# First expert's last weight piece split in two blocks, and the second expert's first eight gathers issued in one run

## The chip, the core and the metric

One NeuronCore of a Trainium2 chip runs the whole kernel. Its engines are TensorE (PE, with its weight loads as PEld), VectorE (DVE), ScalarE (ACT), GpSimd (POOL) and SyncE (SP, which only issues transfers here). Each engine runs its own instructions strictly in the order in which the program lists them, and waits for the others through semaphores. The metric is the device time of one execution in microseconds; the time given for a kernel is the median of its timed runs.

## What is computed

A decayed (retention) attention over 4 batches, 8 heads, 768 positions and head size 64, whose output is read as 3072 tokens of 512 numbers, and then a mixture of 8 experts in which each token goes to the expert with the highest logit:

```python
def _moe_ref(x, w_gate, w_output_gate, w1, w2):       # x: 3072 x 512, the attention's output
    logits = x @ w_gate
    e_idx = np.argmax(logits, axis=1)
    ...                                               # gate_w: the softmax of the chosen expert; eom: an output gate
    for e in range(E):
        mask = e_idx == e
        h = np.maximum(x[mask] @ w1[e], 0.0)
        ye = h @ w2[e]
        out[mask] = gate_w[mask, None] * eom[mask, e, None] * ye
```

Everything is in float32, and the experts' products are made to that accuracy.

## The kernel before

**Precision.** An expert's matrix product is three TensorE products: each operand is held as a high part (`...hi`, rounded to TensorE's fast float32 form) and a low part (`...lo`, the rest), and `mm3` (lines 85 to 87) adds hi x hi, lo x hi and hi x lo. So each block of weights, of tokens and of hidden values is split before use: ACT makes the high part (`split_hi`, line 132, tile `whi`; `x_hi`, line 982, `xhi`; the relu of line 1061, `hhi`), and DVE the low part by a subtraction (`split_lo2`, line 146, `wlo`; `x_lo`, line 986, `xlo`; line 1062, `hlo`).

**Weights.** An expert's two matrices come as four pieces of 1 MB (`load_piece`, line 119, tile `raw`, three buffers): pieces 0 and 1 are the halves of the first expert's w1, pieces 2 and 3 those of its w2, piece 4 the first of the second expert. In this document a piece's tiles carry its number: `wlo_2` is the low part of piece 2. `split_lo2(i, h)` makes half h of piece i's low part. SP issues a piece when its buffer is free.

**Tokens.** The experts are ordered by how many tokens they got. Each expert's tokens are fetched from DRAM by gathers on POOL (`gather`, line 951: one indirect DMA of 128 rows for each 32 tokens, tile `xg`), whose row numbers DVE makes (`row_index`, lines 920 and 925, from an index table that SP loads); DVE turns them (`x_turn`, line 968, tile `y`), and the split makes `xhi` and `xlo`. The second expert needs 14 gathers.

**The first expert.** Its tokens come in two parts, columns 0 to 191 (`h = 0`) and 192 to 447 (`h = 1`), since the last tokens are routed late. The hidden values are 8 chunks (fc = 0 to 7) of 12 matmuls for each part (tile `ph`), then the output rows (`down_rows_mm`, tile `pyr`) of 24 matmuls for each block of rows: each fc takes one matmul each of `whi`, `wlo` and `hlo` (lines 85, 86, 87), fc 0 to 3 from piece 2 and fc 4 to 7 from piece 3. The work of part 0 is the list `units`; `fill(n)` issues its next n entries on TensorE between other work, and the relus that follow a chunk are kept back until `settle()` issues them. So between `fill` and `settle` calls the code fixes by hand where splits, relus, row numbers and gathers stand on ACT, DVE and POOL; TensorE's own order doesn't depend on it. Lines 1455 to 1478 are that stretch for the end of part 0: it issues the relus of chunks 4 to 7, the splits of piece 3 and the last half of piece 2, the second expert's row numbers and its first six gathers. Then part 1 runs as a loop over fc, in which each step also issues one further gather of the second expert (`next_rows`); ahead of such a gather POOL copies one number out of the step's fresh `hhi` (`pace`, line 913, tile `beat`), so that a gather waits for its step. The two scatters of the first expert's finished rows (`send_rows`, line 1178) stand on POOL too, where `emit_rows` is called.

**The second expert** begins with `ph_None` (all its columns at once), so all of its tokens must be gathered, turned and split by then. From there on each expert's weights and tokens are fetched and split during the one before.

Of the kernel before, what the change touches and what calls it, by code (L numbers as in the profile page):

```python
# [9 lines left out]
F32 = mybir.dt.float32  # L10
# [13 lines left out]
def kernel(  # L24
# [28 lines left out]
    FIRST = 192  # L53
# [67 lines left out]
    def split_hi(i, j):  # L121
        if i >= len(pieces):
            return
        if pieces[i] not in wparts:
            wparts[pieces[i]] = (
                wpool.tile([P, 4, 512], F32R, tag="whi", bufs=4, name=f"whi_{i}"),
                wpool.tile([P, 4, 512], F32R, tag="wlo", bufs=4, name=f"wlo_{i}"),
            )
        src, hi = raws[i][:, j, :], wparts[pieces[i]][0][:, j, :]
        if turned_out(i):  # L130
            src, hi = by_quarter(src), by_part(hi)
        nc.scalar.copy(out=hi, in_=src)  # L132
# [10 lines left out]
    def split_lo2(i, h):  # L143
        sl = slice(2 * h, 2 * h + 2)
        hi, lo = (t[:, sl, :] for t in wparts[pieces[i]])
        nc.vector.tensor_tensor(out=lo, in0=raws[i][:, sl, :], in1=hi.bitcast(F32), op=ALU.subtract)  # L146
# [794 lines left out]
    def gather(p, b0=0, b1=None, rows=NT):  # L941
        if p >= E:
            return
        for b in range(b0, NB[p] if b1 is None else min(b1, NB[p])):
            i, m = x_place(p, b)
            if (p, i) not in xg and p == 0 and i < 2:
                both = wpool.tile([P, 4, 512], F32, tag="whi", bufs=4, name="xg_0")
                xg[(0, 0)], xg[(0, 1)] = both[:, 0, :], both[:, 1, :]
            if (p, i) not in xg:
                xg[(p, i)] = slot(f"xg_{p}_{i}")  # L950
            nc.gpsimd.indirect_dma_start(  # L951
                out=xg[(p, i)][:, m * P : (m + 1) * P],
                out_offset=None,
                in_=x_q[0 : 4 * rows],
                in_offset=bass.IndirectOffsetOnAxis(ap=gis[(p, b)], axis=0),
                bounds_check=4 * rows - 1,
                oob_is_err=False,
            )
# [77 lines left out]
    hts = {}  # L1036
# [222 lines left out]
    def settle():  # L1259
        while acts:  # L1260
            acts.pop(0)()

    def fill(count):
        for _ in range(min(count, len(units))):
            mm, act = units.pop(0)
            mm()
            if act:
                acts.append(act)

    with tc.manual_schedule():  # L1270
# [181 lines left out]
        load_rows(1)  # L1452
        load_outs0()
        expert_regs(2, order_i[:, 2:E], E - 2)
        for h in range(2):
            split_hi(3, 2 * h)
            split_hi(3, 2 * h + 1)
            fill(8)
            settle()
            if h == 0:  # L1460
                split_lo2(2, 1)
        for h in range(2):
            split_lo2(3, h)
            fill(2)
        row_index(1)
        gather(1, 0, 4)
        split_late()
        settle()
        load_piece(5)
# [4 lines left out]
            x_split(0, g, 1)  # L1474
        fill(4)
        settle()
        gather(1, 4, 6)
        fill(8)
        settle()
        assert not units  # L1480
# [15 lines left out]
        for p in range(E):  # L1496
# [5 lines left out]
            for fc in range(NFC):  # L1502
                if p == 0:
                    up(p, fc, 1)
                    next_rows(1, 6 + fc, 7 + fc, hts[(p, fc)][0][0:1, FIRST : FIRST + 1].bitcast(F32))
                    if fc >= 4:
                        next_split(4, (fc - 4,))
                    if fc >= 5:
                        for f in work[:2]:
                            f()  # L1510
                        work = work[2:]
                else:
                    up(p, fc)
                    next_split(4 * p + 2, (fc,))

                    if fc == 1 and p in TURNED:
                        out_index(p)
                    if fc == 3 and p == E - 1:
                        count_over()
                    if fc >= 4:  # L1520
                        for f in work[: (fc - 2) // 2]:
                            f()
                        work = work[(fc - 2) // 2 :]
                if fc == 3 and p in TURNED:
                    down_banks(p)
                if p == 1:
                    b = 4 + (fc if fc < 6 else 2 * fc - 6)
                    next_rows(2, b, b + 1 + fc // 6, hts[(p, fc)][0][0:1, 0:1].bitcast(F32))
                if p > 1 and fc < 4:
                    b = 4 * 2 if p - 1 in TURNED else 3 * 2  # L1530
                    n = (14 - b + 3) // 4
                    next_rows(p + 1, b + n * fc, b + n * fc + n, hts[(p, fc)][0][0:1, 0:1].bitcast(F32))
                if fc == 0:
                    load_outs(p + 1)
                    load_rows(p + 2)
                if p - 1 in TURNED:
                    if fc == 2:
                        fetch_turned(p - 1)
                    if fc >= 5:
                        send_turned(p - 1, fc - 5)  # L1540
# [32 lines left out]
    with tc.If(anyover > 0):  # L1573
        with tc.tile_pool(name="opool", bufs=1) as opool:
            for p in range(E):
                n_p = nc.values_load(over_i[0:1, p : p + 1], min_val=0, max_val=(NT + P - 1) // P - OVER[p])
                e = bass.ds(nc.values_load(order_i[0:1, p : p + 1], min_val=0, max_val=E - 1), 1)
                with tc.For_i(0, n_p, 1) as i:
# [30 lines left out]
                    for half in range(2):  # L1609
                        ph = bank("o_ph")  # L1610
                        for f in range(4):
                            fc = 4 * half + f
# [55 lines left out]
```

## Time and profile before

| | |
|---|---|
| median of 3 timed runs | 425.43 us (422.97, 425.43, 425.44) |
| the profiled execution's own time | 424.38 us |
| its span, first to last instruction | 422.7 us (1.68 us lie around it) |
| TensorE busy | 403.0 us, 95% |
| DVE busy | 286.5 us, 68% |
| POOL busy | 238.5 us, 56% |
| ACT busy | 189.5 us, 45% |
| attention and routing | to about 120 us of the span |
| first expert | about 120 to 174 us |
| seven more experts | about 175 to 419 us |

Times in a trace count from the span's start. A busy share is an average over stages: what a change in one stage is worth is read from the waits in that stage. A timeline row gives an instruction's start, its duration, its engine and line, what it writes and reads, how many instructions the row joins, and in brackets how long the engine had been idle before it and what ended that. In rows the piece and expert numbers of a tile are left out: `wlo` stands for any piece's.

### The profile page before, as it was taken

What the parts mean: (1) busy time and instruction counts of PE and PEld (TensorE: products, weight loads), DVE (VectorE), ACT (ScalarE), POOL (GpSimd) and SP (SyncE); (2) the same over time, 40 slices, a digit from 0 to 9 for tenths busy, and PEclk for the clock granted to TensorE, in tenths of its full rate; (3) what the DMA queues carried; (4) which work ended last, traced back from release to release, by engine and by line L of the source; (5) the groups of instructions that cost most, each with busy time, mean ns of one, the idle gap of its engine ahead of it and who ended that gap; (6) DMA issues with size and microseconds to landing.
All of it is one profiled execution on the core that took longest, in us unless ns stands there. A gap on an engine that the chain in (4) does not pass through costs nothing.

```text
span 422.7 us, 10572 instructions
## 1 busy us (share of the span) xinstructions
PE 403.0 (95%) x3869; PEld 368.1 (87%) x3869; DVE 286.5 (68%) x810; ACT 189.5 (45%) x460; POOL 238.5 (56%) x301
## 2 busy tenths in 40 slices
PE   6999989989999899999999999999999999999994
PEld 3888878878788597799999999999999989989983
DVE  2758696877789536767865966965884874874710
ACT  4766556665574125344324604703633542542400
POOL 5276678658955777567575467457187266211012
PEclk9999999999999999999999999999999999999999
DMA  8989898889925851465458557946865885361001
GB/s 180 226 230 242 221 256 229 213 236 253 358 69 140 268 181 37 139 212 174 136 158 261 191 181 174 341 131 190 287 214 157 265 287 174 126 222 46 5 26 50
DMA packets 95326, 79.11 MB, mean 187 GB/s; under 512 B 58668, under 2 KB 70992, under 8 KB 95264
## 3 DMA queue, kind: packets, MB, share of 16 engines
q1 hardware_dynamic: 88336, 64.88, 52.1%
q0 software_dynamic: 6208, 12.93, 9.7%
q8 instruction: 32, 0.52, 0.5%
q10 hardware_dynamic: 720, 0.53, 0.5%
q14 instruction: 30, 0.25, 0.2%
HBM read 62.25 MB, written 16.45 MB: 186 GB/s over the span
## 4 chain that ended last, share of the span: by engine, by line
PE 81%; DVE 8%; DMA 5%; another core or an unknown queue 1%; issue 1%; ACT 1%; SPq 0%; POOL 0%; POOLq 0%; DVEq 0%; ACTq 0%
PE ph_None L85 10%; PE ph_None L86 10%; PE ph_None L87 9%; PE py L85 6%; PE py L87 6%; PE py L86 6%; PE pyr L86 4%; PE pyr L87 4%; PE pyr L85 4%; PE ps L401 4%; PE po L476 4%; DMA qkv<-in_k_dram 3%; PE pk L342 2%; PE po L426 2%; PE ph L87 2%; PE pq L342 2%
## 5 line engine op out<-in xcount | busy, mean ns | idle before, releaser
L951 POOL DMA_INDIRECT xg<-x_d,rows x100 | 111.3, 1113 | 60.9 <-issue 33.0
L1061 ACT ACTIVATE hhi<-ph_None 128x400 fp32r<-128x400 f32 (+4 forms) x56 | 28.1, 501 | 113.7 <-PE ph_None L87 81.6
L85 PE MATMUL ph_None<-xhi,whi 128*128 128x400 f32 (+4 forms) x224 | 76.4, 341 | 0.9 <-ACT xhi L982 0.9
L132 ACT CAST whi<-raw 128x512 fp32r<-128x512 f32 x128 | 74.7, 617 | 4.2 <-DMA raw<-in_moe_w_dram 4.2
L86 PE MATMUL ph_None<-xlo,whi 128*128 128x400 f32 (+4 forms) x224 | 76.4, 341 | 0.0
L87 PE MATMUL ph_None<-xhi,wlo 128*128 128x400 f32 (+4 forms) x224 | 76.3, 341 | 0.0
L141 DVE TENSOR_TENSOR wlo<-raw,whi 128x512 fp32r<-128x512 f32 x112 | 74.3, 684 | 0.6 <-ACT whi L132 0.5
L1062 DVE SCALAR_TENSOR_TENSOR hlo<-ph_None,hhi 128x400 fp32r<-128x400 f32 (+4 forms) x56 | 31.6, 565 | 39.7 <-ACT hhi L1061 26.4
L85 PE MATMUL py<-hhi,whi 128*128 128x400 f32 (+2 forms) x128 | 44.6, 348 | 0.0
L86 PE MATMUL py<-hlo,whi 128*128 128x400 f32 (+2 forms) x128 | 44.6, 348 | 0.0
L87 PE MATMUL py<-hhi,wlo 128*128 128x400 f32 (+2 forms) x128 | 44.6, 348 | 0.0
L85 PEld LDWEIGHTS ph_None<-xhi,whi 128*128 128x128 f32 x224 | 42.1, 188 | 1.7 <-ACT xhi L982 1.3
L1178 POOL DMA_INDIRECT out_dram<-yn,table x12 | 12.6, 1048 | 53.5 <-DVE yn L1242 36.6
L86 PEld LDWEIGHTS ph_None<-xlo,whi 128*128 128x128 f32 x224 | 42.1, 188 | 0.6 <-DVE xlo L986 0.2
L87 PEld LDWEIGHTS ph_None<-xhi,wlo 128*128 128x128 f32 x224 | 42.1, 188 | 0.3
L411 DVE TENSOR_TENSOR at<-ps,decay 128x512 f32<-128x512 f32 x48 | 31.1, 682 | 13.2 <-PE ps L401 8.8
L86 PE MATMUL pyr<-wlo,hhi 128*128 128x512 f32 (+2 forms) x96 | 37.6, 392 | 1.8 <-DVE wlo L146 1.8
L346 ACT COPY qT<-pq 64x256 f32<-64x256 f32 x96 | 37.7, 393 | 1.7 <-PE pq L342 0.7
L85 PE MATMUL pyr<-whi,hhi 128*128 128x512 f32 (+2 forms) x96 | 37.5, 390 | 0.0
L87 PE MATMUL pyr<-whi,hlo 128*128 128x512 f32 (+2 forms) x96 | 37.4, 390 | 0.0
L713 POOL DMA_INDIRECT tab_d<-rec,idx x24 | 26.6, 1107 | 14.1 <-issue 9.7
L982 ACT CAST xhi<-y 128x256 fp32r<-128x256 f32 (+3 forms) x64 | 19.5, 357 | 31.5 <-DVE y L968 22.4
(237 smaller groups left out, 784.3 us busy)
## 6 DMA issues: line engine op xcount, KB each, us to landing
raw<-in_moe_w_dram SPq DMA_DIRECT2D x32, 1024.0 KB
x_d<-xn SPq DMA_DIRECT2D x22, 256.0 KB
qkv<-in_k_dram SPq DMA_DIRECT2D x40, 128.0 KB
qkv<-in_v_dram SPq DMA_DIRECT2D x20, 256.0 KB
qkv<-in_q_dram SPq DMA_DIRECT2D x36, 128.0 KB
yd<-yo SPq DMA_DIRECT2D x12, 256.0 KB
yr<-yd SPq DMA_DIRECT2D x48, 64.0 KB
xg<-x_d,rows POOLq DMA_INDIRECT x100
```

Of the source, the lines that this page charges most:

```text
L85: nc.tensor.matmul(ps, a[0], b[0], start=first, stop=False)
L86: nc.tensor.matmul(ps, a[0], b[1], start=False, stop=False)
L87: nc.tensor.matmul(ps, a[1], b[0], start=False, stop=last)
L132: nc.scalar.copy(out=hi, in_=src)
L141: eng.tensor_tensor(out=lo, in0=src, in1=hi.bitcast(F32), op=ALU.subtract)
L346: copies = [lambda r=r, view=view, src=src: nc.scalar.copy(out=view(qT[r]), in_=src) for r, view, src in query_parts(pq)]
L411: nc.vector.tensor_tensor(out=at, in0=ps.rearrange("p (g t) -> p g t", g=NPAIR), in1=dec[:, j], op=ALU.mult)
L713: ins = nc.gpsimd.indirect_dma_start(out=tab_d, out_offset=bass.IndirectOffsetOnAxis(ap=idx, axis=0), in_=rec, in_offset=None, bounds_chec ...
L951: nc.gpsimd.indirect_dma_start(out=xg[(p, i)][:, m * P : (m + 1) * P], out_offset=None, in_=x_q[0 : 4 * rows], in_offset=bass.IndirectOffs ...
L982: nc.scalar.copy(out=hi, in_=src)
L1061: nc.scalar.activation(out=hi[:, r], in_=ph[:, r], func=AF.Relu)
L1062: nc.vector.scalar_tensor_tensor(out=lo[:, r], in0=ph[:, r], scalar=0.0, in1=hi[:, r].bitcast(F32), op0=ALU.max, op1=ALU.subtract,)
```

## The change

In the hand-written stretch at the end of part 0, the high parts of piece 3 are now made in one block (four casts) instead of two by two around two relus. The last half of piece 2's low part, and then both halves of piece 3's, now stand on DVE as early as their place in the new order lets them: the former ahead of the low parts of chunks 4 and 5, the latter ahead of those of chunks 6 and 7. The number of entries that `fill` issues is the same, and so is TensorE's order. The second expert's gathers 0 to 7 are issued in one call where 0 to 3 stood; the later call for 4 and 5 is gone, and the paced gathers of the loop are numbers 8 to 13 instead of 6 to 13, one a step from fc = 0.

```diff
@@ -1452,18 +1452,18 @@
         load_rows(1)
         load_outs0()
         expert_regs(2, order_i[:, 2:E], E - 2)
-        for h in range(2):
-            split_hi(3, 2 * h)
-            split_hi(3, 2 * h + 1)
-            fill(8)
-            settle()
-            if h == 0:
-                split_lo2(2, 1)
+        for j in range(4):
+            split_hi(3, j)
+        fill(8)
+        split_lo2(2, 1)
+        settle()
+        fill(8)
         for h in range(2):
             split_lo2(3, h)
-            fill(2)
+        settle()
+        fill(4)
         row_index(1)
-        gather(1, 0, 4)
+        gather(1, 0, 8)
         split_late()
         settle()
         load_piece(5)
@@ -1474,7 +1474,6 @@
             x_split(0, g, 1)
         fill(4)
         settle()
-        gather(1, 4, 6)
         fill(8)
         settle()
         assert not units
@@ -1502,7 +1501,7 @@
             for fc in range(NFC):
                 if p == 0:
                     up(p, fc, 1)
-                    next_rows(1, 6 + fc, 7 + fc, hts[(p, fc)][0][0:1, FIRST : FIRST + 1].bitcast(F32))
+                    next_rows(1, 8 + fc, 9 + fc, hts[(p, fc)][0][0:1, FIRST : FIRST + 1].bitcast(F32))
                     if fc >= 4:
                         next_split(4, (fc - 4,))
                     if fc >= 5:
```

On DVE, at the end of part 0 (`hlo_4` to `hlo_7` are the low parts of chunks 4 to 7, the `wlo` rows are `wlo_2`'s last half and the two halves of `wlo_3`; the numbers behind the names only tell buffers apart):

```order
-L1062 SCALAR_TENSOR_TENSOR hlo_4_2974<-ph_4_0_2947,hhi_4_2973 128x192
-L1062 SCALAR_TENSOR_TENSOR hlo_5_2978<-ph_5_0_2960,hhi_5_2977 128x192
 L146 TENSOR_TENSOR wlo_2830<-raw_2413,whi_2829 128x1024
-L1062 SCALAR_TENSOR_TENSOR hlo_6_3011<-ph_6_0_2984,hhi_6_3010 128x192
-L1062 SCALAR_TENSOR_TENSOR hlo_7_3015<-ph_7_0_2997,hhi_7_3014 128x192
+L1062 SCALAR_TENSOR_TENSOR hlo_4_2977<-ph_4_0_2949,hhi_4_2976 128x192
+L1062 SCALAR_TENSOR_TENSOR hlo_5_2981<-ph_5_0_2962,hhi_5_2980 128x192
 L146 TENSOR_TENSOR wlo_2944<-raw_2598,whi_2943 128x1024 x2
+L1062 SCALAR_TENSOR_TENSOR hlo_6_3013<-ph_6_0_2984,hhi_6_3012 128x192
+L1062 SCALAR_TENSOR_TENSOR hlo_7_3017<-ph_7_0_2997,hhi_7_3016 128x192
```

Piece 3's low part no longer stands behind the low parts of chunks 6 and 7, which wait for ACT's relus, but ahead of them.

On POOL, the gathers of the first expert's last tokens (`xg_2` and `xg_3` of lines 133 and 134), then those of the second expert and the two scatters, before:

```order
L951 DMA xg_3_2862<-x_d,rows_1_2844 128x128
L951 DMA xg_0_3040<-x_d,rows_0_3035 128x128 x4
L1178 DMA out_dram<-yn_0_3099,table_0_2884 3072x512
L951 DMA xg_1_3104<-x_d,rows_0_3035 128x128 x2
L1178 DMA out_dram<-yn_1_3123,table_0_2884 3072x512
L913 COPY beat<-hhi_0_2811 1x1
L951 DMA xg_1_3104<-x_d,rows_0_3035 128x128
L913 COPY beat<-hhi_1_2815 1x1
L951 DMA xg_1_3104<-x_d,rows_0_3035 128x128
```

and after the change:

```order
L951 DMA xg_3_2862<-x_d,rows_1_2844 128x128
L951 DMA xg_0_3040<-x_d,rows_0_3035 128x128 x4
L951 DMA xg_1_3053<-x_d,rows_0_3035 128x128 x4
L1178 DMA out_dram<-yn_0_3112,table_0_2884 3072x512
L1178 DMA out_dram<-yn_1_3129,table_0_2884 3072x512
L913 COPY beat<-hhi_0_2811 1x1
L951 DMA xg_2_3150<-x_d,rows_0_3035 128x128
L913 COPY beat<-hhi_1_2815 1x1
L951 DMA xg_2_3150<-x_d,rows_0_3035 128x128
```

Eight gathers now stand ahead of the two scatters, and the last paced gather is that of fc = 5, where it was that of fc = 7. On ACT the four casts of `whi_3` now stand together ahead of the relus of chunks 4 and 5, where two of them stood behind these. SP's order is the same.

## Rows read from the trace of the kernel before

**Rows 1.** Windows: stretch, its length, busy us (instructions) by engine, clock, DMA.

```profile
core 0: us, PE busy (x) PEld busy (x) DVE busy (x) ACT busy (x) POOL busy (x), PEclk, DMA share, GB/s
...
160.00:163.20 3.20, 2.20 (x15) 1.67 (x14) 0.42 (x1) 0.91 (x3) 1.27 (x3) 1.00 0.14 41
...
174.20:176.00 1.80, 0.94 (x4) 0.66 (x4) 1.34 (x5) 1.27 (x5) 0.00 (x0) 1.00 0.12 36
176.00:422.70 246.70, 240.45 (x1294) 230.60 (x1293) 163.22 (x425) 95.42 (x210) 120.94 (x135) 1.00 0.54 173
```

**Rows 2.** Waits of TensorE, 118 to 176 us: total, times, longest.

```profile
PE pyr L86 <- DVE wlo L146: 1.8, 1, 1.8
PE ph_None L85 <- ACT xhi L982: 0.9, 1, 0.9
```

**Rows 3.** Timeline of TensorE, from 139 us.

```profile
139.61 0.39 PE L85 MATMUL pyr<-whi,hhi 128*128 128x512 f32 x1
141.76 0.50 PE L86 MATMUL pyr<-wlo,hhi 128*128 128x512 f32 x1 [1.76 <-DVE wlo L146]
...
149.95 0.28 PE L85 MATMUL ph<-xhi,whi 128*128 128x256 f32 x1
...
173.88 0.39 PE L87 MATMUL pyr<-whi,hlo 128*128 128x512 f32 x1
175.13 0.47 PE L85 MATMUL ph_None<-xhi,whi 128*128 128x432 f32 x1 [0.86 <-ACT xhi L982]
```

**Rows 4.** Timeline of DVE in the same stretch.

```profile
136.35 0.58 DVE L1062 SCALAR_TENSOR_TENSOR hlo<-ph,hhi 128x192 fp32r<-128x192 f32 x2
136.86 1.21 DVE L146 TENSOR_TENSOR wlo<-raw,whi 128x1024 fp32r<-128x1024 f32 x1
...
140.22 0.36 DVE L1062 SCALAR_TENSOR_TENSOR hlo<-ph,hhi 128x192 fp32r<-128x192 f32 x1 [1.79 <-ACT hhi L1061]
140.49 2.35 DVE L146 TENSOR_TENSOR wlo<-raw,whi 128x1024 fp32r<-128x1024 f32 x2
142.86 0.23 DVE L920 SCALAR_TENSOR_TENSOR rowf<-index 32x16 f32<-32x16 int32 x1
...
144.73 0.70 DVE L968 STREAM_TRANSPOSE y<-xg 128x512 f32<-128x512 f32 x1
148.19 0.31 DVE L968 STREAM_TRANSPOSE y<-xg 128x128 f32<-128x128 f32 x1 [2.76 <-DMA xg<-x_d,rows]
148.90 1.03 DVE L986 TENSOR_TENSOR xlo<-y,xhi 128x160 fp32r<-128x160 f32 x4 [0.39 <-issue]
...
174.25 0.45 DVE L968 STREAM_TRANSPOSE y<-xg 128x256 f32<-128x256 f32 x1 [2.00 <-DMA xg<-x_d,rows]
```

**Rows 5.** Timeline of ACT in the same stretch.

```profile
133.37 1.14 ACT L132 CAST whi<-raw 128x512 fp32r<-128x512 f32 x2 [4.20 <-DMA raw<-in_moe_w_dram]
...
139.85 0.33 ACT L1061 ACTIVATE hhi<-ph 128x192 fp32r<-128x192 f32 x1 [1.82 <-remote]
...
162.29 0.39 ACT L1061 ACTIVATE hhi<-ph 128x256 fp32r<-128x256 f32 x1 [3.86 <-remote]
```

**Rows 6.** Timeline of POOL in the same stretch: gathers.

```profile
137.26 1.70 POOL L951 DMA_INDIRECT xg<-x_d,rows  x1 [0.31 <-issue]
...
140.57 2.00 POOL L951 DMA_INDIRECT xg<-x_d,rows  x1 [0.30 <-issue]
142.88 1.00 POOL L951 DMA_INDIRECT xg<-x_d,rows  x1 [0.30 <-DMA x_d<-xn]
144.77 0.99 POOL L951 DMA_INDIRECT xg<-x_d,rows  x1 [0.89 <-PE pyr L87]
...
168.76 1.04 POOL L951 DMA_INDIRECT xg<-x_d,rows  x1 [0.16 <-issue]
```

**Rows 7.** Timeline of SP's queue: the loads of pieces 5, 6 and 7.

```profile
143.37 0.25 SPq L119 DMA_DIRECT2D raw<-in_moe_w_dram  x1
...
144.94 24.02 SPq L119 DMA_DIRECT2D raw<-in_moe_w_dram  x2
```

## The prediction

> **What bounds the kernel now.** I read the busy shares first: TensorE is busy for 95% of the span. The windows say where the rest is. From 176 us to the end it is busy for 240.45 of 246.70 us at a granted clock of 1.00, the 2.4 GHz level [rows 1], so there it is the bound, and what it gains ahead of 175.13 should pass to the end one for one. The waits of TensorE, taken over the first expert alone, then show two that are long: 1.8 us of a `pyr` matmul for `wlo`, and 0.9 us of the first `ph_None` matmul for `xhi` [rows 2]. The timelines place them.
>
> The first is at 141.76: `pyr` at fc = 4 needs the first half of `wlo_3` and idles for 1.76 us [rows 3]. DVE makes both halves of it in the row at 140.49, behind a `hlo` (chunk 7's) that started at 140.22 after 1.79 us of idling for its `hhi` [rows 4]. ACT could start that relu only at 139.85, after an idle time that ended with a signal from elsewhere ("remote") [rows 5]. Nothing that `wlo_3` needs came so late: the casts of `whi_3` began at 133.37 and the relus and casts around them take 0.5 to 0.6 us each [rows 5]. Order alone held it up.
>
> The second is at 175.13: `xhi` waits for `y`, which DVE starts at 174.25 after 2.00 us of waiting for a gather [rows 3, 4]. That is the second expert's last one, which POOL issued at 168.76 [rows 6], beside the load of piece 7, which SP issued in the row that ends at 168.96 [rows 7].
>
> **What the stalls cost.** From start to start the first is 141.76 - 139.61 = 2.15 us. A matmul takes 240.45 / 1294 = 0.19 us on average in the long stretch [rows 1], so 1.96 us are lost, and 1.76 are if only the idle time counts. The first matmul after it takes 0.11 us more than the one ahead (0.50 and 0.39) [rows 3]. I take 2.0. The second is 175.13 - 173.88 - 0.19 = 1.06, and after it three new matmuls fill the 0.87 us up to 176.00 [rows 1], 0.29 each where 0.19 is usual: 0.3 more. I take 1.3.
>
> **The splits in their new order.** Nothing is removed or added here; all is moved. ACT makes four casts from 133.37, about 0.57 each (1.14 for two) [rows 5], to 135.7, and the relus of chunks 4 and 5 to 136.2 at the latest, as early as DVE comes to need them: it is at other work up to 136.35 [rows 4]. Then it makes `wlo_2`'s last half first (1.21, to 137.6, where it ended at 138.07), `hlo_4` and `hlo_5` (0.58, to 138.2), `wlo_3` (2.35 for two, so halves at 139.3 and 140.5), and `hlo_6` and `hlo_7` (0.36 for one, to 141.2) [rows 4]. TensorE wants the first half one matmul after 139.61, at 139.8: not late, by half a microsecond. At about 0.2 us for each matmul and three for each fc it wants `hlo_6` eight matmuls after 139.61, at 141.2, and gets it at 140.9; it wants `hlo_7` at 141.8 and gets it at 141.2. So the wait goes and no other of its size is next to it: **2.0 us** on TensorE, if the tokens after it keep up.
>
> **The first expert's last tokens** are what is late next. Part 1 starts at 149.95 [rows 3] and would start at 147.95. Its `xhi` and `xlo` come from a `y` at 148.19 that waited 2.76 us for a gather; the first `xlo` starts at 148.90 and the four take 1.03 [rows 4]. That gather is POOL's at 142.88. Its two neighbours at 137.26 and 140.57 took 1.70 and 2.00 us where others take 1.00 [rows 6], and just these started with the `wlo` subtractions of 136.86 and 140.49 under way or about to start [rows 4]. In the new order these subtractions are gone after 140.5. I estimate half of the 1.7 us back, so that the last gather starts at about 141.9, and ends at 142.9, ahead of SP's issue of piece 5 at 143.37 [rows 7] and not behind it. A gather that ended at 142.57 had landed by 144.73, since `y` then started without waiting [rows 4, 6]: at most 2.2 us. So `y` can start at about 145.2; 0.71 later the first `xlo` starts, and TensorE needs it no earlier than 147.95. Hidden. The other bound is a `y` that stays at 148.19: then the four `xlo` end at 149.93 as before, part 1 is held for most of the time that it gained, and I put what is left of the 2.0 at 1.2, since part 1's first products use only parts that are made first.
>
> Here a rule of the Trainium skill bears on the same point. On its page "SBUF — State Buffer", section "Who interferes with whom", a subtraction with both inputs in SBUF takes only the read side of the port pair that DVE shares with GpSimd, and the page infers that making descriptors needs the write side, so the two would not meet. By that clause the gather comes no earlier and the sum is that of the rival below at 422.9; the rows of 1.70 and 2.00 against 1.00 us speak for the other reading, by which the sum is 422.1.
>
> **The gathers in one run.** No gather is added. Eight on end from 144.77, at 1.30 each (0.99 and 0.30 between them), end at 155.2; the scatters behind them, with two more steps, at 157.8. They only write finished rows, and nothing of this expert waits for them. Six paced gathers follow at about 1.4 each (1.04, 0.16 and the copy), the last issued at about 164.8 instead of 168.76 [rows 6], if its `hhi` is there: that of fc = 4 is relued at 162.29 [rows 5] and fc = 5 comes a chunk later, so about 163.5. With the 5.5 us of the last gather before (168.76 to 174.25) `y` starts at 170.3 at the latest, with 3.2 (1.0 and the bound of 2.2) at 168. From `y` to the first `ph_None` matmul are 0.88 us, and TensorE, now 2.0 earlier, arrives at 171.9 to 172.1: `y` is due at 171.1. Hidden: **1.3 us** more. If POOL kept its old place, this stall would grow by the 2.0 of the first. So the two parts need each other.
>
> **Sum.** 424.38 - 2.0 - 1.3 = 421.1 against the profiled execution, which lies 1.05 below the median of 425.43. So the median should be **422.1 us**.
>
> **The rivals.**
>
> The gather of the last tokens lands when it did. For it: its landing of over 4 us after its end (143.88 to 148.19) can have other causes than piece 5's load. Then 1.2 and 1.3 are kept, 2.5: **422.9**. Chance 0.2.
>
> TensorE gains more. Inside part 1 it is busy for only 2.20 of 3.20 us at 160 us, and ACT's relu at 162.29 had waited 3.86 us there [rows 1, 5]. If these delays hang on POOL's paced gathers beside them, and vanish, another 1.0 to 1.8 us go: **420.3**. Against it: the row names no POOL instruction, and TensorE doesn't wait for POOL there. Chance 0.12.
>
> The other sign: the subtractions catch the gathers of the first expert instead of leaving them. Three halves now lie close together, and each can add up to 1.0 to a gather that starts with it (2.00 against 1.00 [rows 6]). If that pushes the last one 1.4 us back, it is issued behind piece 5, at 143.37, with piece 6 right behind (144.94) [rows 7]; if it then shares with both, `y` comes at about 151.3 instead of 148.19. Part 1 then starts near 152, 2 us later than before, and 1.3 from the second expert come off: +0.7, **426.1**. It decides from a `y` later than about 149.5 on. Against it: the three halves are done by 140.5, and only two gathers started ahead of that. Chance 0.1.
>
> TensorE's signals to ACT come late in several places (1.82 and 3.86 us of idling ended by "remote" [rows 5]). If the relu of chunk 7 comes a microsecond later still, `hlo_7` is late and most of the gain is lost again: **425.0**. Chance 0.08.
>
> The run of gathers holds DVE. By the same section of the skill, whoever comes first holds the shared pair for the whole instruction and the other waits; as a mechanism here, each of up to four `xlo` would wait out a gather of 1.3, so up to 5.2 us on part 1's tokens, 5.2 - 3.3 over the time before: **427.3**. The rows speak against it: four `xlo` took 1.03 together while such gathers ran on POOL [rows 4, 6]. Chance 0.03.
>
> **How the numbers follow.** The forecast holds 0.47, and the rivals 0.2, 0.12, 0.1, 0.08 and 0.03 in this order. The three timed runs lie 2.47 apart, so about 1% (4.3 us) is what a measurement of this kernel tells from no change. The range from 420.3 to 425.6 takes in the forecast, the first, second and fourth case, 0.87 together; their edges and the spread of the runs take that to about 0.8. Faster by over 1% means under 421.2: nearly all of the second rival and a little of the forecast, 0.14. Slower by over 1% means over 429.7: no case reaches it but the mishaps of the third and fifth, 0.04. The rest is 0.82.
>
> **What the profile after would show.** For the first step: no wait of `pyr` for `wlo`, and `wlo` x2 on DVE ended by 140.6 ahead of `hlo`. For the second: the first expert's last gather before 142.5, `y` without a wait of 2.76 us, and part 1's first matmul near 148.0. For the third: the last gather of the second expert near 165, and `ph_None` begun near 172 without a wait for `xhi`. The forecast is wrong if `y` of the last tokens still starts after 148, if `hlo_7` takes the place of `wlo_3` in TensorE's waits, or if the stretch from 176 us on is no longer the same 247 us that it was.

## The result, and the profile after

| | before | after |
|---|---|---|
| timed runs side by side, median (lowest to highest) | 423.53 us (421.58 to 430.42), 12 runs | 428.09 us (425.47 to 431.16), 12 runs |
| ratio after to before, 95% interval | | 1.0109 (1.0081 to 1.0138) |
| the profiled execution's own time | 424.38 us | 427.46 us |
| its span | 422.69 us | 425.86 us |
| part 1 of the first expert, first to last matmul | 149.95 to 163.20: 13.25 us | 147.42 to 166.79: 19.37 us |
| first `ph_None` matmul | 175.13 | 178.21 |

The change made the kernel 1.1% slower, where 0.8% faster was forecast. Both stalls that it aims at are gone, and part 1, which stood in no term of the sum, takes 6.1 us more.

The timeline of TensorE in the changed kernel:

```profile
139.18 0.39 PE L85 MATMUL pyr<-whi,hhi 128*128 128x512 f32 x1
139.41 0.39 PE L86 MATMUL pyr<-wlo,hhi 128*128 128x512 f32 x1
...
147.42 0.28 PE L85 MATMUL ph<-xhi,whi 128*128 128x256 f32 x1
...
155.63 0.38 PE L87 MATMUL ph<-xhi,wlo 128*128 128x256 f32 x1 [0.26 <-issue]
...
157.05 0.28 PE L85 MATMUL ph<-xhi,whi 128*128 128x256 f32 x1 [0.69 <-issue]
...
157.78 0.28 PE L85 MATMUL ph<-xhi,whi 128*128 128x256 f32 x1 [0.21 <-issue]
158.50 0.37 PE L86 MATMUL ph<-xlo,whi 128*128 128x256 f32 x1 [0.45 <-issue]
...
159.20 0.28 PE L85 MATMUL ph<-xhi,whi 128*128 128x256 f32 x1 [0.21 <-issue]
159.92 0.37 PE L86 MATMUL ph<-xlo,whi 128*128 128x256 f32 x1 [0.44 <-issue]
...
161.33 0.37 PE L86 MATMUL ph<-xlo,whi 128*128 128x256 f32 x1 [0.81 <-issue]
162.74 0.37 PE L87 MATMUL ph<-xhi,wlo 128*128 128x256 f32 x1 [1.04 <-issue]
...
178.21 0.35 PE L85 MATMUL ph_None<-xhi,whi 128*128 128x432 f32 x1
```

The `pyr` matmul of fc = 4 that waited at 141.76 [rows 3] follows its neighbour at 139.41 without a pause, part 1 starts 2.53 us earlier than at 149.95 [rows 3], and the first `ph_None` waits for nothing. But from 155 us on TensorE pauses again and again, and the profile names nobody whom it waits for ("issue"). The waits of TensorE from 118 to 176 us say the same (total, times, longest); the two rows of before [rows 2] are gone from the list:

```profile
PE ph L86 <- issue: 1.7, 3, 0.8
PE ph L87 <- issue: 1.3, 2, 1.0
PE ph L85 <- issue: 1.1, 3, 0.7
```

The windows of part 1 and what follows (columns as in [rows 1]):

```profile
147.42:155.37 7.95, 7.95 (x66) 7.74 (x64) 1.59 (x3) 0.77 (x2) 6.12 (x7) 1.00 0.74 246
155.37:161.00 5.63, 2.90 (x15) 2.15 (x15) 0.42 (x1) 0.74 (x2) 4.83 (x8) 1.00 0.32 95
161.00:167.80 6.80, 5.19 (x20) 4.53 (x20) 3.50 (x7) 2.50 (x7) 3.63 (x7) 0.50 0.10 29
167.80:178.21 10.41, 10.41 (x48) 8.60 (x46) 9.38 (x25) 5.31 (x14) 3.97 (x4) 1.00 0.39 122
```

TensorE runs 65 matmuls of part 1 in the first 7.95 us (the 66th of the row is a `pyr` that ends there), then only 15 in 5.63 us, and after that idling its granted clock falls to 0.50, the 1.2 GHz level, for the next 6.8 us.

What went before the pauses shows on ACT, whose relus of part 1 wait for TensorE's signal that a chunk is done:

```profile
149.05 0.38 ACT L1061 ACTIVATE hhi<-ph 128x256 fp32r<-128x256 f32 x1 [2.96 <-issue]
151.37 0.38 ACT L1061 ACTIVATE hhi<-ph 128x256 fp32r<-128x256 f32 x1 [1.93 <-PE ph L87]
155.66 0.38 ACT L1061 ACTIVATE hhi<-ph 128x256 fp32r<-128x256 f32 x1 [3.91 <-PE ph L87]
160.64 0.38 ACT L1061 ACTIVATE hhi<-ph 128x256 fp32r<-128x256 f32 x1 [4.60 <-remote]
164.23 0.38 ACT L1061 ACTIVATE hhi<-ph 128x256 fp32r<-128x256 f32 x1 [3.20 <-PE ph L87]
```

A chunk is 12 matmuls of 0.12 us, so relus should come 1.44 us apart. The first is on time; the next come 2.32, 4.29, 4.98 and 3.59 us apart, although ACT is idle and TensorE has issued its matmuls without a gap up to 155.4. Chunk 2 (36 matmuls) was issued by 151.9 and its relu ran at 155.66. The signal is late, not the issue of the work. And on POOL (gathers on L951, scatters on L1178):

```profile
141.29 1.00 POOL L951 DMA_INDIRECT xg<-x_d,rows  x1 [0.30 <-issue]
144.20 0.99 POOL L951 DMA_INDIRECT xg<-x_d,rows  x1 [1.92 <-DVE rows L925]
...
156.08 0.94 POOL L1178 DMA_INDIRECT out_dram<-yn,table  x1 [0.30 <-issue]
...
157.33 1.06 POOL L951 DMA_INDIRECT xg<-x_d,rows  x1 [0.16 <-issue]
...
158.73 1.05 POOL L951 DMA_INDIRECT xg<-x_d,rows  x1 [0.16 <-issue]
...
160.12 1.03 POOL L951 DMA_INDIRECT xg<-x_d,rows  x1 [0.16 <-issue]
...
161.88 1.02 POOL L951 DMA_INDIRECT xg<-x_d,rows  x1 [0.55 <-issue]
164.74 0.18 POOL L913 COPY beat<-hhi 1x1 f32<-1x1 f32 x1 [1.84 <-ACT hhi L1061]
...
167.09 1.02 POOL L951 DMA_INDIRECT xg<-x_d,rows  x1 [0.16 <-issue]
```

From 144.20 POOL issues 14 indirect DMAs with no more than 0.8 us between any two, up to 162.9. Of TensorE's eight restarts, those at 157.05, 158.50, 159.92 and 161.33 lie 0.03 to 0.18 us behind the ends of the rows of 156.08, 157.33, 158.73 and 160.12, but those at 155.63, 157.78, 159.20 and 162.74 lie inside an indirect DMA. The longer steps of TensorE are all 1.41 to 1.45 us, also from 161.33 to 162.74, where POOL's step was 1.76 us (160.12 to 161.88). So the rows tie the pauses to the stretch in which POOL issues, not to its single DMAs. That gave the theory for the experiments.

**Theory A:** while POOL issues indirect DMAs without a pause, TensorE's completion signals come through slowly; TensorE goes on issuing until about 32 matmuls are unsignalled, and then runs at the pace of the signals. (32 is an estimate, counted from the matmul and relu rows. When the pauses began 65 matmuls of part 1 had been issued and 24 to 36 signalled, so 29 to 41 were out; in the kernel before, at its first pause of 0.43 us, 84 and 48 to 60, so 24 to 36.) **Theory B:** TensorE stops by itself, because it no longer gets the pause of 1.76 us ahead of part 1.

### The profile page after: what moved, and what is told of

The parts are those of the page before. It is cut to its first block, busy times and chain, and to the rows that moved or that the text cites. A ratio compares the mean times of both kernels' runs of the same rounds, so it can differ in the third digit from the quotient of the medians.

```text
span 425.9 us, 10567 instructions
## 1 busy us (share of the span) xinstructions
PE 408.0 (96%) x3869; PEld 372.1 (87%) x3869; DVE 284.1 (67%) x810; ACT 189.4 (44%) x460; POOL 235.8 (55%) x299
## 4 chain that ended last, share of the span: by engine, by line
PE 88%; DVE 5%; DMA 3%; issue 2%; ACT 0%; POOL 0%; POOLq 0%; DVEq 0%; SPq 0%
PE ph_None L87 9%; PE ph_None L86 9%; PE ph_None L85 9%; PE py L87 6%; PE py L85 6%; PE py L86 6%; PE pyr L85 5%; PE pyr L86 5%; PE pyr L87 5%; PE ps L401 5%; PE po L476 4%; PE pk L342 3%; PE po L426 3%; PE pq L342 2%; PE pst L489 2%
## 5 line engine op out<-in xcount | busy, mean ns | idle before, releaser
L951 POOL DMA_INDIRECT xg<-x_d,rows x100 | 111.1, 1111 | 67.4 <-issue 35.1
L1178 POOL DMA_INDIRECT out_dram<-yn,table x12 | 12.6, 1048 | 50.5 <-DVE yn L1242 33.3
```

The costliest lines, as they stand in the source:

```text
L951: nc.gpsimd.indirect_dma_start(out=xg[(p, i)][:, m * P : (m + 1) * P], out_offset=None, in_=x_q[0 : 4 * rows], in_offset=bass.IndirectOffs ...
```

## The experiments

The clock's level and TensorE's pauses are told from one profiled execution each, the times from runs beside the kernel before. Each run of part 1 is 96 matmuls; undisturbed it takes 11.51 us, as will be seen. The runs were made in five sets, each beside runs of the kernel before, and in the third and fifth that kernel itself was about 2% faster (416.3 and 415.5 us; 425.7, 425.3 and 422.7 in the others). That turned out to be part of the answer. A ratio is taken over the runs side by side, with its 95% interval, and need not be the quotient of the two medians.

**Half of the change each.** With the splits alone:

```diff
-        gather(1, 0, 8)
+        gather(1, 0, 4)
...
+        gather(1, 4, 6)
...
-                    next_rows(1, 8 + fc, 9 + fc, hts[(p, fc)]...)
+                    next_rows(1, 6 + fc, 7 + fc, hts[(p, fc)]...)
```

> The splits of the change alone: the gathers stay as in the kernel before (four in one run, two more later, the paced ones from number 6). Theory A (POOL's indirect DMAs): while POOL issues indirect DMAs one behind the other, TensorE's completion signals come through slowly, and after some thirty matmuls that are not yet signalled TensorE stops; what counts is how long POOL's unbroken run lasts beside part 1. Here POOL has 12 of them from about 144 us to the copy that waits for fc = 4, not 14 as in the changed kernel: part 1 starts at about 147.4, loses 3 to 6 us (11.5 us undisturbed; 19.4 in the changed kernel, 13.4 before), time 423 to 426. Theory B (TensorE's own doing: the missing pause of 1.76 us ahead of part 1 is what makes it stall): part 1 takes 19 us as in the changed kernel, time 427 to 429.

Measured: 426.45 us, ratio 1.0020 (0.9980 to 1.0059). Part 1:

```profile
147.11:163.66 16.55, 14.30 (x98) 13.27 (x97) 5.37 (x11) 4.00 (x10) 11.76 (x16) 0.90 0.44 145
```

The gathers alone are the same edit on the kernel before, the other way round.

> The gathers of the change alone: the splits stay as in the kernel before, with the pause of 1.76 us for wlo. Theory A: POOL's unbroken run is two gathers longer than before, part 1 starts at about 150 as before and loses 3 to 6 us instead of 2; the wait for the second expert's tokens (1.3 us) goes; time 423 to 427. Theory B: part 1 is no slower than before (about 13.4 us), and the wait at its end goes: 422.3.

Measured: 429.65 us (4 runs), ratio 1.0103 (1.0015 to 1.0191). In its profile part 1 started at 153.03, since the wait of `pyr` for `wlo` was 2.6 us there and cost a stretch of half clock as well, and took 14.28 us. Both times lie above what theory A gave (423 to 426 and 423 to 427), though both losses in part 1 don't: 5.04 us for the splits, within the 3 to 6 expected, and 2.77 for the gathers, just short of them. So each half makes part 1 longer than 13.25 us, and neither is faster. The splits keep their 2 us at its start and give 3.3 back in it; TensorE is 2.8 us earlier there, so more of part 1 lies beside POOL's run. The gathers alone keep the pause and are slower all the same, which speaks against B.

**Part 1 without gathers.** All 14 gathers wait for chunk 7:

```diff
-        gather(1, 0, 8)
...
-                    next_rows(1, 8 + fc, 9 + fc, hts[(p, fc)]...)
+                    if fc == 7:
+                        next_rows(1, 0, 14, hts[(p, fc)]...)
...
-                    if fc >= 5:
-                        for f in work[:2]:
-                            f()
-                        work = work[2:]
```

With the gathers the turns and splits of their tokens (`work`) leave part 1 too.

> The changed kernel with all 14 gathers of the second expert held back until chunk 7 of part 1 is done, so that only the two scatters and no gather run on POOL beside part 1. The second expert must then wait for its tokens, so the total is no measure; part 1 is. Theory A: part 1 starts at about 147.4 and takes 11.5 to 12 us without gaps of TensorE, relus at most 0.3 us behind their chunk's last matmul, granted clock 1.00 up to its end; ph_None starts at about 179 to 182. Theory B: gaps from about 155 us on and half clock as in the changed kernel, 19 us.

```profile
148.10:159.61 11.51, 11.51 (x98) 11.51 (x96) 5.42 (x11) 4.21 (x10) 1.96 (x2) 1.00 0.50 170
```

No pause, all relus 1.44 us apart, full clock. B falls: this kernel has no pause ahead of part 1 either. (`ph_None` waited until 182.94, about as was expected; 435.54 us.) And signals were late in this very execution. The first expert's own gathers run on POOL until 142.93, and beside them the relu of part 0's chunk 7 runs 4.05 us after the chunk's last matmul, which ended at 137.23:

```profile
136.96 0.27 PE L87 MATMUL ph<-xhi,wlo 128*128 128x192 f32 x1
```

```profile
141.28 0.33 ACT L1061 ACTIVATE hhi<-ph 128x192 fp32r<-128x192 f32 x1 [2.26 <-remote]
```

That relu tells for each profile whether signals were late in it: it runs 2.35 to 4.05 us late in every profile of the first, second and fourth sets, and 0.03 to 0.53 us in every one of the third and fifth.

**POOL busy without DMA.** The same with 24 `nc.gpsimd.memset(blank, 0.0)` where the run of gathers stood.

> As the run without gathers beside part 1, but POOL clears an unused tile 24 times (0.52 us each, some 12.5 us from about 142 us on) where the run of gathers stood. If it is POOL being busy, or its port, that holds TensorE's signals, part 1 shows gaps and takes over 14 us. Theory A as stated (indirect DMAs, not work on POOL): 11.5 to 12 us, no gaps, the same as without the clearing.

Measured: 11.51 us, relus on time, POOL busy for 8.49 of it. The relu of part 0's chunk 7 was 2.43 us late here too. So work on POOL by itself does no harm.

**The same rows by another engine.** Two plain loads of 128 rows of 512 bytes after each relu:

```diff
+                    for k in (2 * fc, 2 * fc + 1):
+                        nc.scalar.dma_start(spare_t[k // 4][:, ...], x_q[k * P : (k + 1) * P])
```

> As the run without gathers beside part 1, but ACT issues 16 plain loads beside it, two after each relu, each of 128 rows of 512 bytes, the rows and the size of a gather. If the small rows on the DMA engines hold TensorE's signals, part 1 shows gaps and takes over 14 us. Theory A as sharpened so far (it is POOL issuing indirect DMAs): part 1 takes 11.5 to 12 us, no gap, relus on time.

Measured: 11.52 us, no pause, though part 0's chunk 7 had its relu 2.35 us late; one relu of part 1 was 0.48 us late, behind ACT's own issuing. So small rows on the DMA engines do no harm either. (A plain DMA issued by POOL was not tried.)

**Thinned.** Four gathers in a run, one for each chunk behind its `hhi`, three after chunk 7, scatters last (`kept` holds the two `send_rows` of part 0):

```diff
-        gather(1, 0, 8)
+        gather(1, 0, 4)
...
-                    next_rows(1, 8 + fc, 9 + fc, hts[(p, fc)]...)
+                    next_rows(1, 4 + fc, 5 + fc if fc < 7 else 14, hts[(p, fc)]...)
...
+            if p == 0:
+                for f in kept:
+                    f()
             row_index(p + 2)
```

> The changed kernel's splits, but POOL's work beside part 1 is thinned: four of the second expert's gathers in one run, then one for each chunk, each behind the copy of that chunk's hhi, the last three after chunk 7, and the first expert's two scatters only after these. So a gather of a step can't start before TensorE's signal of that step has come through, and POOL pauses when signals are late. Theory A (TensorE's completion signals are held up while POOL issues indirect DMAs without a pause): part 1 starts at 147.4, its relus come at most 1.5 us late, it has gaps of under 1 us in all and ends at 159 to 160 at full clock; the last gather goes out at about 164, ph_None starts at 170 to 172, and the time is 419 to 422. If it isn't the unbroken run that matters, but any gather beside part 1 costs its share (14 gathers and scatters cost 8 us in the changed kernel, 8 would cost 4 to 5): part 1 ends at 163 and the time is 424 to 426.

Measured: 420.82 us (6 runs) against 425.25, ratio 0.9858 (0.9806 to 0.9911; the quotient of the medians is 0.990): faster than the kernel before, while the changed one was slower than it. Its part 1 and the relus of chunks 3 to 5:

```profile
150.60:162.11 11.51, 11.51 (x97) 11.51 (x96) 5.60 (x11) 4.22 (x10) 8.78 (x14) 1.00 0.52 179
```

```profile
156.55 0.38 ACT L1061 ACTIVATE hhi<-ph 128x256 fp32r<-128x256 f32 x1 [1.06 <-issue]
158.45 0.38 ACT L1061 ACTIVATE hhi<-ph 128x256 fp32r<-128x256 f32 x1 [1.52 <-PE ph L87]
159.43 0.38 ACT L1061 ACTIVATE hhi<-ph 128x256 fp32r<-128x256 f32 x1
```

One signal is late by half a microsecond and the next is on time again: POOL waited for the late one, and so made room. Gathers beside part 1 don't cost by their number. With the scatters left ahead of the paced gathers:

> As the run with late scatters, but the two scatters stay where the change has them, ahead of the paced gathers. Four gathers and two scatters then run from 144 to 152 without a pause, and the paced gathers behind them are two steps late, so that they wait for no signal at first. Theory A: part 1 loses 2 to 4 us, time 421 to 424, between the run with late scatters and that of the splits alone (426.45, where 16.55 us went into part 1). If every gather or scatter costs its share, as with late scatters or 1 us more.

Measured: 422.22 us, ratio 0.9942 (0.9913 to 0.9971); part 1 took 12.28 us, with relus up to 3.9 us apart. Expected and measured agree on the order of the two; the 2 to 4 us were too many, as part 1 lost 0.77. The rest of the difference lies elsewhere: its first `ph_None` waited 1.4 us for tokens, which the thinned kernel's didn't.

**A set in which nothing was late.** Four more kernels: the run of eight with nothing behind it until chunk 5, the kernel before's splits with the thinned order, and the run without gathers beside part 1 with 12 gathers into unused tiles, of 128 and of 32 rows, put in:

```diff
+        for k in range(12):
+            nc.gpsimd.indirect_dma_start(out=spare_t[k // 4][0:128, ...], in_=x_q, ...)
```

> The changed kernel with its run of eight gathers, but nothing on POOL behind it until chunk 5 of part 1: the other six go out two a step at chunks 5, 6 and 7, each pair behind the copy of the step's hhi, and the two scatters after them. POOL's unbroken run is 8 (144.2 to 154.6) and not 14. Theory A with its limit (TensorE goes on until some 32 matmuls are not yet signalled, which the changed kernel reached at 155.1): TensorE is just short of stopping; part 1 takes 11.5 to 12.5 us, its relus of chunks 2 to 4 are 2 to 5 us late and come together at about 156, the clock stays at 1.00; time 419 to 423. If gathers cost in proportion to their number, part 1 takes 15 to 16 us and the time is 424 or more.

> The kernel before's splits with the thinned POOL order of the run with late scatters (420.82): it undoes the split part alone, where part 1 is undisturbed. If the split part is worth what the prediction put on it, this is 2.0 us slower than that run: 422 to 424, with the 1.76 us wait of pyr for wlo back and part 1 at about 11.5 us. If the split part brings nothing, 420 to 421.

> As the run without gathers beside part 1 (its own 14 come after chunk 7), with 12 further gathers of 128 rows into unused tiles in one run where the changed kernel's eight stand, the two scatters behind them: the suspected cause put back alone, 14 indirect DMAs from 144 to about 162. Theory A: part 1 stalls again, 16 to 20 us with gaps and half clock. If it was something else in the order of the second expert's own gathers, splits or turns, part 1 stays at 11.5 us.

> As the run with 12 spare gathers, each of 32 rows instead of 128. If each indirect DMA instruction costs, whatever its rows: part 1 as slow as with 128 rows (16 to 20 us). If the rows cost (what POOL writes for each of them, or what the DMA engines do with it): under 13 us.

Measured: part 1 took 11.51 us in all four. The run of eight had ratio 1.0062 (1.0028 to 1.0095), the old splits 0.9988 (0.9949 to 1.0028), against 416.30 for the kernel before. For the 128-row gathers:

```profile
147.66:159.17 11.51, 11.51 (x97) 11.51 (x96) 5.41 (x11) 4.21 (x10) 8.88 (x9) 1.00 0.50 167
```

Fourteen indirect DMAs on end, and every signal on time. As it stood, A was wrong here: something that differs from set to set decides whether signals are late at all. In these profiles `pyr` didn't wait for `wlo` either, even with the old splits, where the relu of chunk 7 was on time (133.58, its last matmul ended at 133.54).

**Side by side once more.** The kernel before, the changed one and both spare-gather kernels, unchanged, in one set:

> The kernel before once more, beside the others of this call, since the chip of the last call ran it in 416.3 us, not 425, and showed no late signal of TensorE in any of its four kernels, not even beside fourteen indirect DMAs on end. If this chip is like that one: pyr waits for wlo not at all or under 0.5 us (hhi of chunk 7 on time), part 1 takes 11.5 us, time near 416. If it is like the others: relus of part 1 up to 5 us late, 13 us, time near 425.

> The changed kernel once more. Theory A, narrowed: the change's loss is made by late signals of TensorE beside POOL's run, and these come on some chips only. On a chip where the kernel before has its relus on time, the changed kernel has part 1 in 11.5 us, no wait for wlo to gain, only the wait for the last tokens of the second expert (0.9 to 1.3 us): 0 to 1.3 us faster, ratio 0.997 to 1.000. On a chip with late relus: ratio 1.005 to 1.015 as measured first. If on a chip with relus on time the change is still 1% slower, late signals are not its cause.

> The 12 spare gathers of 128 rows again. On a chip where the kernel before has late relus: Theory A gives part 1 in 16 to 20 us with half clock; if part 1 stays at 11.5 us there, the run of gathers alone is not the cause and something in the order of the second expert's own gathers is. On a chip with relus on time it says nothing new (11.5 us).

> The 12 spare gathers of 32 rows again. On a chip with late relus: as slow as with 128 rows if each indirect DMA instruction costs, under 13 us if its rows do. On a chip with relus on time: 11.5 us.

This set had late signals. Changed to before: 427.87 to 422.74 us, ratio 1.0142 (1.0106 to 1.0178). Part 1 of the kernel before and of the changed one:

```profile
151.96:164.36 12.40, 12.13 (x98) 11.66 (x96) 4.84 (x11) 3.90 (x10) 8.63 (x12) 1.00 0.31 102
```

```profile
147.95:166.43 18.48, 14.89 (x97) 13.29 (x96) 3.38 (x8) 2.87 (x8) 12.95 (x18) 0.86 0.41 133
```

and of the spare gathers with 128 and with 32 rows:

```profile
149.29:169.10 19.81, 14.65 (x97) 14.01 (x96) 4.71 (x10) 4.01 (x10) 11.63 (x12) 0.83 0.40 129
```

```profile
147.02:170.96 23.94, 16.45 (x98) 15.15 (x96) 5.24 (x11) 3.99 (x10) 9.96 (x11) 0.71 0.24 78
```

The run of gathers alone, put into a kernel that had part 1 in 11.51 us without it (in the first set; it wasn't run again in this one), brings the whole loss back. A quarter of the rows makes it no smaller: a gather of 32 rows still takes POOL 0.90 us, and the instructions stand closer. So, in one profile of each, what counts is the indirect DMA instruction on POOL, not what it moves.

**The last set** asked what the splits alone are worth beside late signals, with the thinned order and new splits, the run of eight, and the thinned order with old splits.

> The thinned POOL order (four gathers in a run, one for each chunk behind its hhi, scatters last) with the changed splits, beside the next two on one chip. On a chip with late relus, Theory A: part 1 at 11.5 to 12 us, ratio to the kernel before 0.98 to 0.99 as first measured (0.9858). On a chip with relus on time: 0.995 to 1.002. If it is at 1.00 where relus are late, the gain of the first measurement was not the thinning.

> The run of eight with nothing behind it until chunk 5, scatters late. On a chip with late relus, Theory A with the limit of some 32 unsignalled matmuls: relus of chunks 1 to 4 up to 5 us late and then together, TensorE just short of stopping, part 1 at 11.5 to 12.5 us, clock 1.00, ratio 0.983 to 0.993, no better than the thinned order. If gathers cost by their number there, part 1 is at 15 us and the ratio over 0.995. On a chip with relus on time: 1.006 as first measured.

> The kernel before's splits with the thinned POOL order. On a chip with late relus: the wait of pyr for wlo is back (1.8 to 2.6 us) and the time is 1.5 to 3 us above that of the thinned order with the changed splits, ratio 0.986 to 0.995; that difference is what the split part is worth. On a chip with relus on time: no wait for wlo, no difference (0.999 as first measured).

Signals were on time again, on the same chip as in the second set, where they had been late; so it isn't the chip alone. Ratios to 415.48 us, in this order: 1.0009 (0.9983 to 1.0036), 1.0036 (1.0010 to 1.0062) and 1.0011 (0.9976 to 1.0045); part 1 at 11.51 or 11.52 us each time. TensorE at fc = 4 with the old splits:

```profile
135.78 0.39 PE L85 MATMUL pyr<-whi,hhi 128*128 128x512 f32 x1
136.00 0.48 PE L86 MATMUL pyr<-wlo,hhi 128*128 128x512 f32 x1
```

No pause at the place where [rows 3] has 1.76 us. Where signals are on time, neither the new splits nor the thinned order gain anything, since what they mend isn't there.

## Why the prediction was wrong

- **The sum, closed from the rows.** Part 1 starts 2.53 us earlier; it takes 6.12 more; from its end to the first `ph_None` are 11.42 us instead of 11.93, so 0.51 less; from there to the end 247.65 instead of 247.56. -2.53 + 6.12 - 0.51 + 0.09 = 3.17 = 425.86 - 422.69.
- **The first stall, 2.0: right.** TensorE was 0.43 us ahead before it (139.18, and 139.61 in [rows 3]) and 2.53 behind it: 2.10. DVE did it as forecast, `wlo` first and `hlo` after:

```profile
137.60 2.35 DVE L146 TENSOR_TENSOR wlo<-raw,whi 128x1024 fp32r<-128x1024 f32 x2
139.86 0.35 DVE L1062 SCALAR_TENSOR_TENSOR hlo<-ph,hhi 128x192 fp32r<-128x192 f32 x1
140.71 0.36 DVE L1062 SCALAR_TENSOR_TENSOR hlo<-ph,hhi 128x192 fp32r<-128x192 f32 x1 [0.50 <-issue]
...
144.16 0.89 DVE L968 STREAM_TRANSPOSE y<-xg 128x512 f32<-128x512 f32 x2
145.45 1.03 DVE L986 TENSOR_TENSOR xlo<-y,xhi 128x160 fp32r<-128x160 f32 x4 [0.39 <-ACT xhi L982]
```

  But "order alone held it up" was half the cause. The order made `wlo` wait for a late relu. The relu at 139.85 [rows 5] ran 2.88 us after its chunk's last matmul had ended, at 136.97; that is the same late signal, and where it is on time the old order costs nothing.
- **The first expert's last tokens: right, and so the rival that they land as before falls.** Their last gather started at 141.29 (141.9 forecast) and `y` had no wait, where [rows 4] has 2.76 us. Two gathers beside the subtractions took 1.18 and 1.33 us, not 1.70 and 2.00. The Trainium skill's inference, on the page "SBUF — State Buffer", section "Who interferes with whom", that such a subtraction doesn't meet the making of descriptors would have left them where they were; the rows went the other way.
- **The second stall, 1.3: it went, but whether the moved gathers took it away can't be read.** `ph_None` waits for no token, yet TensorE came 6 us later than the 171.9 to 172.1 of the forecast, so the tokens had all the time they needed. The stall isn't a constant of the kernel before either: in its second profile (fourth set) no such wait stands, and from the end of part 1 to the first `ph_None` are 10.91 us (164.36 to 175.27) where the first has 11.93. That 1.02 agrees with the 1.06 read for the wait. The last gather went out at 167.09, not 164.8, behind a copy that waited for the late `hhi` of chunk 4.
- **The step that failed** stands in the part on the gathers in one run: that POOL's work is free for TensorE because nobody waits for its results ("nothing of this expert waits for them"), and with it the tacit zero for part 1. What the runs showed in its place is that, wherever signals were late at all, an unbroken run of indirect DMAs beside part 1 held up TensorE's completion signals (relus up to 9.8 us late in the changed kernel) until TensorE stopped: 18.5 and 19.4 us for part 1 in the changed kernel, 19.8 with the run alone put back, 11.51 without it. Part 1 lost 13.25 - 11.51 = 1.74 us before and 7.86 after. Of the 7.86, 4.34 are pauses (19.37 less the 15.03 that its window has busy) and 3.52 slower matmuls, a little over half of it at half clock (16 matmuls take 3.80 us busy from 162.74 on, where 1.92 is the undisturbed time).
- **The rivals.** The second had the right place and the right suspect, POOL's DMAs beside part 1, and the wrong sign: it asked what would come if the delays vanished, not what a longer run does to them. The fourth saw late signals, but looked for their price at `hlo_7`, not at TensorE itself. The rows were there: 3.86 us of idling on ACT that ended by "remote" [rows 5] and a window with 1.0 us of idle TensorE [rows 1], beside POOL's run. The third (426.1) and the fifth (427.3) come nearest to 428.09 in number, and that is chance: `y` came at 144.16, not late, and four `xlo` took 1.03 us as before.
- **The base.** The three runs of the kernel before had a median of 425.43; twelve gave 423.53. That moves both sides alike and isn't why the sign was wrong.

## What to carry to other kernels

Beside a fast run of small matmuls, don't put a long unbroken run of indirect DMAs on GpSimd, even when no one waits for what they fetch; pace each by a result of the step that runs beside it, so that GpSimd pauses as soon as TensorE's signals lag (with the new splits, 0.9858 of the time in this kernel, and no loss shown where signals are on time). In a profile, a consumer that is idle for microseconds after its producer's last matmul is a finding to be explained before anything is moved, not a constant. And run the kernel before again beside every comparison: here it took 416 or 425 us depending on the set, and the first stall, 2 us of the 3.3 that were to be had, came and went with that in the profiles that have its splits.

## What the runs showed of the hardware

TensorE's completion signals can lag its matmuls by many microseconds beside a run of indirect DMAs on GpSimd, and for some 3 us after it, and then come together. The first relus of part 1 beside the gathers of 32 rows:

```profile
154.58 0.39 ACT L1061 ACTIVATE hhi<-ph 128x256 fp32r<-128x256 f32 x1 [8.94 <-remote]
163.04 0.94 ACT L1061 ACTIVATE hhi<-ph 128x256 fp32r<-128x256 f32 x3 [8.07 <-remote]
```

Part 1 began at 147.02 there, so the first relu was due at 148.65 (1.63 us later, as in the changed kernel) and the second at 150.1. The latter ran 13 us late, at once with the next two, 3.0 us after the run's last indirect DMA had ended at 160.04. TensorE stops when about 32 matmuls are out, by the estimate above. The Trainium skill, on the page "TensorE: Matmul & The Clock Gate", in the part "What happens when you issue a matmul", has a 64-deep window in which TensorE pulls weight loads ahead of matmuls in flight. By an estimate from that figure 32 pairs of the two would fill it, but no run here shows that it is that window.

Open is what makes signals late in one set and not in the next. It is neither the kernel (the same kernel had both) nor the chip alone (one chip had both). Something else goes with it: the traces of all 13 profiles with late signals hold about 5,400 to 5,900 semaphore updates, those of the seven with signals on time about 8,300 to 8,500, for nearly the same program, and most of the missing ones tell of landed DMAs. Whether that is a sign of the same cause, and whether the recording of a trace has itself a part in the late signals, no run here shows.

Open, too, is what the new splits are worth alone beside late signals with part 1 undisturbed, and how the changed kernel does where signals are on time: no run here had these together. Why the run of eight is 0.4% to 0.6% slower where signals are on time, although part 1 takes 11.51 us, is open in part: in its two profiles TensorE needs the same 240.41 us from the first `ph_None` to its last matmul as in the three with the thinned order, but from there to the end are 8.5 and 8.3 us, where they have 6.3 to 7.4. So in these profiles the time is lost behind the last matmul; by what isn't shown.
